# Banded attention in a gated mix kernel: the band as a 0/1 multiply by GpSimd in place of a mask matmul, in attention steps 4 to 11

## The chip, the core and the metric

The kernel runs on one core of one Trainium2 chip. The metric is the time of one execution in device microseconds (us), lower is better. Instructions of the five engines are named as the profile names them: PE is TensorE's matmul and PEld its weight load, DVE is VectorE, ACT is ScalarE, POOL is GpSimd, SP is SyncE, which here only issues DMAs. L596 is line 596 of the kernel before.

## What is computed

Two branches are mixed by a gate. Branch A is a long causal convolution by FFT (H3), branch B is a dilated sliding-window attention: each query sees 8 keys, at distances 0, 2, ..., 14, in 32 heads of 20 columns. The change lies in branch B. Cut to that:

```
def _B_ref(x, wqkv, wo):
    B, S, D = x.shape                    # 1, 2048, 640
    H = 32; Dh = D // H
    W, dil = 8, 2
    qkv = (x @ wqkv) split into q, k, v of H heads
    idx = arange(S)[:, None] - (arange(W) * dil)[None, :]
    mask = idx >= 0
    logits = einsum("bhsd,bhswd->bhsw", q, k[idx]) * Dh ** -0.5
    attn = softmax(where(mask, logits, -1e9))
    o = einsum("bhsw,bhswd->bhsd", attn, v[idx])
    return o.reshape(B, S, D) @ wo

g = sigmoid((A_q * gate_w).sum(-1))
return g * _A_ref(A_q, ...) + (1 - g) * _B_ref(A_q, B_wqkv, B_wo)
```

## The kernel before, in words

**Tiling of the attention.** Even and odd positions are separate sequences, so that the dilated window becomes 8 neighbouring keys. Each sequence is cut into blocks of 57 queries (QB) with the 64 keys (KB) that they can see. For every block and head a 64 x 57 square of scores is computed, of which only a diagonal band of 8 keys per query counts. What lies outside the band has to be made zero before the product with v.

**The unit of work.** A *half* is two heads (of a group of four, t = 0 to 7) over 6 pairs of blocks (a group of blocks, gi = 0 to 2). There are 48 halves, two to a *step*, 24 steps, in the order of `steps` (L575): the groups 0 and 1 with t = 0, 1, then 2, 3, then 4 to 7, and then group 2. For half i, `scores(i)` (L581) issues on PE two mask matmuls of 128 x 342 (L587), whose product of two small factors `mk` and `mq` is 0 in the band and at most -256 outside of it, then 24 score matmuls of 20 rows x 57 columns (L593) that add the scores to it in PSUM tile `sc` (two buffers). ACT then takes the exponential of the 128 x 684 tile into one of four buffers `ET` (L596): outside the band that gives zero. `pv(i)` (L598) multiplies it with v, whose extra column of ones gives the sum for the softmax, in 24 matmuls (L615) into PSUM tile `O` (one buffer); after the second half of a step DVE divides (L622, L625).

**The order of the work.** All of it is written by hand; every engine runs its own instructions in program order and waits on semaphores for the others. In loop k (L703) the order is: `scores(2k+2)`, `fill(0)`, `scores(2k+3)`, `fill(1)`, `pv(2k)`, `fill(2)`, `pv(2k+1)`, `fill(3)`. So the exponentials of a step are needed one loop later. `fill` spreads other work of PE, given by `plan` (L694), over the four places: for k = 0 to 7 the projection of q and k for the other heads (`late_qk`, 5 or 4 units of five matmuls, L349), for k = 8 to 11 that of v (`late_v`, 3 units, L292), from k = 12 on the output projection and the first FFT stages.

**What else hangs on this stage.** On DVE `kv_gen` (L244), the elementwise part of branch A, goes on until k = 2; its last instructions are L257 and L259 (tile `kvo`). When it is done, the tile `kq1` takes the place of what `kv_gen` read (`new_kq(1)`, L752); heads 20 to 31 are moved into it by `send_rest(ft)` (L356), 28 DMAs on SP's queue: ft = 0 to 2 at once (17 DMAs), ft = 3 and ft = 4 when their projection is done, with two loads `hn` of 512 KB (L522) put in between (`load_hn`, L758 and L759). These heads are used from t = 5 on, that is from half 18. GpSimd is nearly empty: small DMAs at the start (L227 to L239), four memsets (L571), 12 small stores and 4 loads of the gate (L725), and output stores at the end.

Of the kernel before, what the change touches and what calls it, by code (L numbers as in the profile page):

```python
# [11 lines left out]
BF = mybir.dt.bfloat16  # L12
F32 = mybir.dt.float32
ACT = mybir.ActivationFunctionType
ALU = mybir.AluOpType
# [4 lines left out]
D = 640  # L20
L = 4096
H = 32
DH = 20
NDT = 5
SCALE = float(DH) ** -0.5

QB = 57
KB = 64
CB = QB + KB
# [7 lines left out]
NMB = 6  # L37
# [5 lines left out]
def _np_bf16(a):  # L43
    return np.asarray(a, dtype=np.float32).astype(ml_dtypes.bfloat16)
# [32 lines left out]
def attn_consts():  # L77
    B, C = 256.0, 512.0
    kk = np.arange(KB); qq = np.arange(QB)
    kc = kk // 8 - 4; ko = kk % 8; qc = qq // 8 - 4; qo = qq % 8  # L80
    sk = np.where(kc % 2 == 0, 1.0, -1.0); sq = np.where(qc % 2 == 0, 1.0, -1.0)
    mk = np.zeros((NF, KB)); mq = np.zeros((NF, QB))
    mk[0] = kc * kc; mk[1] = kc; mk[2] = 1.0
    mq[0] = -B; mq[1] = B * (2 * qc + 1); mq[2] = -B * (qc * qc + qc) - C / 2
    for v in range(8):
        mk[3 + v] = sk * (ko == v)
        mq[3 + v] = (C / 2) * sq * np.where(v < qo, -1.0, 1.0)
    tot = np.einsum("fk,fq->kq", mk, mq)
    dlt = kk[:, None] - qq[None, :]
    inb = (dlt >= 0) & (dlt <= 7)  # L90
    assert (tot[inb] == 0).all() and (tot[~inb] <= -C / 2).all()
    for m in (mk, mq):
        assert (_np_bf16(m).astype(np.float64) == m).all()
    mkz = np.zeros((4, 32, 128)); mqz = np.zeros((4, 32, NMB * QB))
    mkz[:, 0:NF] = np.tile(mk, (1, 2)); mqz[:, 0:NF] = np.tile(mq, (1, NMB))
    sidx = 2 * np.arange(18)[None, :] + (np.arange(128)[:, None] // KB)
    pos = QB * (sidx % NSB) - PRE + (np.arange(128)[:, None] % KB)
    valid = ((pos >= 0) & (pos < 1024)).astype(np.float32)
    return dict(mk=_np_bf16(mkz.reshape(128, -1)), mq=_np_bf16(mqz.reshape(128, -1)), valid=_np_bf16(valid), ident=_np_bf16(np.eye(128)))


def xrow(si, kk):
# [32 lines left out]
def kernel(  # L135
# [14 lines left out]
    nc = tc.nc  # L150
# [8 lines left out]
    ca = {k: nc.inline_tensor(v, name=f"ca_{k}") for k, v in attn_consts().items()}  # L159
# [6 lines left out]
    ident = p0.tile([128, 128], BF, name="ident")  # L166
# [16 lines left out]
    pC = sC.enter_context(tc.tile_pool(name="pC", bufs=1, side="left", reuse_waits="tile"))  # L183
    xTn = pC.tile([128, NDT, 2, XP], BF, name="xTn")
    Wp = pC.tile([128, NDT, 2, NDT, 4, 32], BF, name="Wp")
    WV = pC.tile([128, NDT, D + 8], BF, name="WV")
    valid = pC.tile([128, 18], BF, name="valid")
    sV = ExitStack()
    pV = sV.enter_context(tc.tile_pool(name="pV", bufs=1, side="left", reuse_waits="tile"))
    wl = pV.tile([128, 4, D], BF, name="wl")  # L190
# [46 lines left out]
    nc.gpsimd.dma_start(F1b[:], cf["F1b"].ap())  # L237
    nc.gpsimd.dma_start(mk[:], ca["mk"].ap())
    nc.gpsimd.dma_start(mq[:], ca["mq"].ap())  # L239


    kvs = kv_scr[:]
# [324 lines left out]
    NET = 4  # L567
    ETs = []
    for e in range(NET):
        ETb = pD.tile([128, 2, 352], BF, name=f"ET{e}")  # L570
        nc.gpsimd.memset(ETb[:, :, NMB * QB:352], 1.0)  # L571
        ETs.append(ETb)
    pa_ = ExitStack()
    ppa = pa_.enter_context(tc.tile_pool(name="ppa", bufs=2, space=PSUM, reuse_waits="tile"))
# [6 lines left out]
    def scores(i):  # L581
        gi, t, hf = halves[i]
        kqt = kq[t // 4]
        sc = ppa.tile([128, 2, 512], F32, name="sc", tag="sc")
        for hh in range(2):
            r = 32 * (2 * hf + hh)
            nc.tensor.matmul(sc[:, hh, 0:NW], lhsT=mk[:], rhs=mq[:], start=True, stop=False, skip_group_check=True)  # L587
        for mb in range(NMB):
            for sub in range(2):
                si = 2 * (NMB * gi + mb) + sub  # L590
                for hh in range(2):
                    r = 32 * (2 * hf + hh)
                    nc.tensor.matmul(sc[64 * sub:64 * sub + 64, hh, QB * mb:QB * mb + QB], lhsT=kqt[r:r + DH, t % 4, si, 0:KB],  # L593
                                     rhs=kqt[r:r + DH, t % 4, si, KB:CB], start=False, stop=True,
                                     tile_position=(r, 64 * sub), skip_group_check=True)
        nc.scalar.activation(ETs[i % NET][:, :, 0:NW], sc[:, :, 0:NW], ACT.Exp, scale=SCALE)  # L596

    def pv(i):  # L598
        gi, t, hf = halves[i]
        if hf == 0:  # L600
            Ot = ppa.tile([128, 2, 512], F32, name="O", tag="O", bufs=1)
            Os[(gi, t)] = Ot
            if t == 0:
                oSb = pD.tile([128, 2, 3, D], BF, name="oS", tag="oS", bufs=2)
                oSs[gi] = oSb
        O = Os[(gi, t)]
        ET = ETs[i % NET]
        for mp in range(3):
            for hh in range(2):
                for par in range(2):  # L610
                    for s in range(2):
                        mb = 2 * mp + par
                        sl = mp * 4 + 2 * hf + hh
                        rows = slice(64 * s, 64 * s + 64)
                        nc.tensor.matmul(O[64 * par:64 * par + 64, s, 21 * sl:21 * sl + 21],  # L615
                                         lhsT=ET[rows, hh, QB * mb:QB * mb + 64],
                                         rhs=VW[rows, NMB * gi + mb, 4 * t + 2 * hf + hh, :], start=True, stop=True,
                                         tile_position=(64 * s, 64 * par), skip_group_check=True)
        if hf == 1:
            Ov = O[:, :, 0:252].rearrange("p a (s e) -> p a s e", e=21)  # L620
            rd = pD.tile([128, 2, 12], F32, name="rd", tag="rd", bufs=2)
            nc.vector.reciprocal(rd[:], Ov[:, :, :, DH])  # L622
            for s in range(2):
                dst = oSs[gi][:, s, :, 4 * DH * t:4 * DH * (t + 1)].rearrange("p b (h d) -> p b h d", h=4)
                nc.vector.tensor_tensor(dst, Ov[:, s, :, 0:DH].rearrange("p (b h) d -> p b h d", h=4),  # L625
                                        rd[:, s].rearrange("p (b h) -> p b h", h=4).unsqueeze(3).to_broadcast([128, 3, 4, DH]),
                                        ALU.mult)
# [75 lines left out]
    for k in range(len(steps)):  # L703
        late_eng[:] = "aa" if k < 5 else "da"
        if k == 12:
            gl = gate()
            sC.close()
            pF = ctx.enter_context(tc.tile_pool(name="pF", bufs=1, side="left", reuse_waits="tile"))
            kv = pF.tile([128, 2, 64, 80], BF, name="kv")
            G = pF.tile([128, 32, 2, 128], BF, name="G")  # L710
            for c in range(2):
                for h in range(2):
                    for q in (0, 2, 1, 3):
                        paced.append((kv[32 * q:32 * q + 32, c, 32 * h:32 * h + 32],
                                      raw(kvs, (2 * q + c) * S * 80 + 2560 * h, [[64 * 80, 32], [1, 2560]])))
            for a_ in range(0, 32, 8):
                for q in (0, 2, 1, 3):
                    paced.append((G[32 * q:32 * q + 32, a_:a_ + 8],
                                  cf["G"].ap()[32 * q:32 * q + 32, a_ * 256:a_ * 256 + 2048].rearrange("p (a r b) -> p a r b", a=8, r=2)))
            fg["s"] = itertools.chain(s1_gen(("h", 0), 0, True), s1_gen(("h", 1), 1, True))  # L720
        if k == 12:
            fg["o"] = op_gen(0)
        if k == 14:
            for a_ in gl:
                nc.gpsimd.dma_start(*a_)  # L725
        if k == 16:
            fg["p"] = op_gen(1)
        units = [c for c, n in plan.get(k, []) for _ in range(n)]
        cut = [len(units) * j // 4 for j in range(5)]

        def fill(j):
            for c in units[cut[j]:cut[j + 1]]:
                advance(fg[c], 1)

        nxt = k + 1 < len(steps)
        if nxt:
            scores(2 * k + 2)
        fill(0)
        if nxt:
            scores(2 * k + 3)  # L740
        fill(1)
        pv(2 * k)
        fill(2)
        pv(2 * k + 1)
        fill(3)
        if k < KC:
            advance(kvg, 3)
        if k == KC - 1:
            while advance(kvg, 1):
                pass  # L750
            sV.close()
            new_kq(1)  # L752
            for ft in range(2 + sum(plan[k_][0][1] for k_ in range(KC)) // 12):
                send_rest(ft)
            hb = p0.tile([128, 16 * D], BF, name="hb", tag="hT")
            hT = hb[:].rearrange("p (g m i) -> p g m i", g=NG, i=IL)
            bl = hb[:].rearrange("p (t d) -> p t d", d=D)
            load_hn(0)  # L758
            load_hn(1)  # L759
        if k > 8:  # L760
            advance(ht, 2 if k < 16 else 3)
# [155 lines left out]
```

## Time and profile before

| what | value |
|---|---|
| time, median of 4 runs | 302.88 us (301.67, 302.47, 303.29, 305.65) |
| the profiled execution | 301.67 us |
| its span, first to last instruction | 299.9 us |
| mean granted TensorE clock | 0.916 |
| PE busy | 245.8 us, 82% |
| DVE busy | 196.6 us, 66% |
| ACT busy | 180.4 us, 60% |
| GpSimd busy | 26.6 us, 9% |
| PE busy from 72 to 111 us, loops 3 to 10 | 37.22 of 39.00 us |
| ACT, DVE, GpSimd busy in the same stretch | 20.16, 20.25, 0.00 us |
| mask matmuls, L587 | 96, 22.9 us busy |

Times in the profile are counted from the span's start. Busy time of PE overlaps, because matmuls are pipelined: what an instruction costs is read from where the next one starts, not from its duration. An engine's idle time is put down to what ended it ("<-"). GpSimd's durations are rough.

### The profile page before, as it was taken

How to read it: one execution, taken by the hardware profiler on the slowest of the kernel's cores; microseconds unless marked ns; L12 is line 12 of the kernel's file. 1: busy time of each engine (PE TensorE's matmuls, PEld its weight loads, DVE VectorE, ACT ScalarE, POOL GpSimd, SP SyncE). 2: the span in 40 equal slices, each digit the busy share in tenths (PEclk: the TensorE clock that was granted, in tenths of full speed). 3: DMA queues.
4: the chain of work that ended last, by engine and by line, in shares of the span. 5: the costliest groups of instructions: out<-in, count | busy, mean ns of one | idle time of the engine just before them, and what ended most of it. 6: DMA issues, size and time to landing. Idle time of an engine off the chain costs nothing. (4 is left out here: it accounts for less than half of the span.)

```text
span 299.9 us, 12166 instructions
## 1 busy us (share of the span) xinstructions
PE 245.8 (82%) x5502; PEld 177.6 (59%) x5502; DVE 196.6 (66%) x294; ACT 180.4 (60%) x275; POOL 26.6 (9%) x52
## 2 busy tenths in 40 slices
PE   2788999999999979987699987899787969597420
PEld 1556766566566646654456654587676969497310
DVE  2587999299343668757497554025868877985771
ACT  2366788666655444542245653398778977975860
POOL 3820004100000001320000000000000000000232
PEclk9999999999999999996959999599889979979655
DMA  6999905120556630464622324562855949491273
GB/s 190 357 357 406 341 2 156 46 91 2 126 94 121 134 45 21 101 169 119 145 66 65 107 63 128 153 154 68 195 166 116 240 83 242 106 256 40 71 198 90
DMA packets 19162, 42.22 MB, mean 141 GB/s; under 512 B 4263, under 2 KB 11767, under 8 KB 18102
## 3 DMA queue, kind: packets, MB, share of 16 engines
q1 hardware_dynamic: 17606, 39.19, 47.7%
q0 software_dynamic: 1504, 2.24, 3.1%
q8 instruction: 43, 0.70, 1.1%
q14 instruction: 9, 0.07, 0.1%
HBM read 26.22 MB, written 7.87 MB: 114 GB/s over the span
## 5 line engine op out<-in xcount | busy, mean ns | idle before, releaser
L596 ACT ACTIVATE ET<-sc 128x684 bf16<-128x684 f32 x48 | 35.3, 742 | 25.2 <-PE sc L593 25.0
L349 PE MATMUL pj<-xTn,Wp 128*128 128x349 bf16 (+1 forms) x300 | 49.9, 311 | 0.0
L463 PE MATMUL s<-Am,G 64*128 64x64 bf16 x1280 | 25.6, 197 | 11.1 <-issue 4.9
L349 PEld LDWEIGHTS <-Wp 128*128 128x128 bf16 x300 | 26.6, 97 | 12.8
L122 ACT CAST kq<-pj 128x342 bf16<-128x342 f32 (+1 forms) x54 | 24.0, 473 | 16.6 <-PE pj L349 16.3
L463 PEld LDWEIGHTS <-G 64*128 64x128 bf16 x1280 | 22.7, 100 | 15.1 <-issue 9.7
L496 DVE TENSOR_TENSOR Hb<-Up,Hb 128x1024 bf16<-128x1024 bf16 x40 | 25.1, 686 | 4.3 <-ACT Up L122 1.8
L122 ACT CAST Am<-s 128x1024 bf16<-128x1024 f32 x25 | 24.7, 1040 | 3.8 <-PE s L439 3.7
L652 PE MATMUL op<-wo,oT 128*128 128x320 bf16 x120 | 22.5, 327 | 5.0 <-ACT oT L639 2.2
L122 ACT CAST Hb<-s 128x1024 bf16<-128x1024 f32 x20 | 20.0, 1020 | 10.5 <-PE s L463 10.3
L509 PE MATMUL i<-M,Hb 128*128 128x128 bf16 x320 | 23.7, 234 | 2.2 <-DVE Hb L496 2.0
L509 PEld LDWEIGHTS <-Hb 128*128 128x128 bf16 x320 | 22.7, 150 | 3.3 <-DVE Hb L496 3.1
L657 DVE CAST fin<-op 128x320 bf16<-128x320 f32 x24 | 11.7, 486 | 19.2 <-PE op L652 12.0
L593 PEld LDWEIGHTS <-kq 20*64 20x64 bf16 x1152 | 13.9, 109 | 16.6 <-issue 15.6
L587 PE MATMUL sc<-mq,mk 128*128 128x342 bf16 x96 | 22.9, 322 | 0.2 <-ACT ET L596 0.2
L250 DVE TENSOR_TENSOR pr<-kvw,wl 128x2560 bf16<-128x2560 bf16 x16 | 22.9, 1486 | 0.1
L615 PEld LDWEIGHTS <-ET 64*64 64x64 bf16 x1152 | 13.9, 111 | 12.4 <-issue 11.5
L593 PE MATMUL sc<-kq 20*64 20x57 bf16 x1152 | 19.4, 195 | 1.8 <-issue 1.3
L292 PEld LDWEIGHTS <-vw 128*128 128x128 bf16 x180 | 16.9, 100 | 6.6
L528 DVE STREAM_TRANSPOSE hb<-hn 128x512 bf16<-128x512 bf16 x20 | 19.9, 1040 | 0.2
L615 PE MATMUL O<-VW,ET 64*64 64x21 bf16 x1152 | 18.6, 182 | 0.1
L625 DVE TENSOR_TENSOR oS<-O,rd 128x240 bf16<-128x240 f32 x48 | 17.3, 403 | 0.9
(71 smaller groups left out, 370.0 us busy)
## 6 DMA issues: line engine op xcount, KB each, us to landing
Hb<-Hb SPq DMA_DIRECT2D x10, 512.0 KB
xN<-in_A_q_dram SPq DMA_DIRECT2D x4, 640.0 KB
kvw<-in_A_k_dram SPq DMA_DIRECT2D x4, 640.0 KB
kv_scr<-kvo SPq DMA_DIRECT2D x4, 640.0 KB
hn<-in_A_ssm_k_dram SPq DMA_DIRECT2D x5, 512.0 KB
kv<-kv_scr SPq DMA_DIRECT2D x16, 160.0 KB
qg<-in_A_q_dram SPq DMA_DIRECT2D x16, 160.0 KB
b_scr<-fin SPq DMA_DIRECT2D x36, 60.0 KB
```

The source lines that it names most:

```text
L122: self.nc.scalar.copy(dst, src)
L250: nc.vector.tensor_tensor(pr[:, j].rearrange("p (n c) -> p n c", n=4), kh[:, 4 * c + 3 - j:4 * c + 7 - j, :], wl[:, j, :].unsqueeze(1).to_ ...
L349: nc.tensor.matmul(ps[:, 0:n], lhsT=Wp[:, dt, which, ft].rearrange("p h c -> p (h c)"), rhs=xTn[:, dt, c // 3, a:a + n], start=(dt == 0), ...
L463: nc.tensor.matmul(o, lhsT=G[rows, j, r, :], rhs=Am[rows, 2 * j + r, :, :], start=(r == 0), stop=(r == 1), tile_position=(64 * c, 0), skip ...
L496: nc.vector.tensor_tensor(blk_(H_), blk_(Up), blk_(H_), ALU.mult)
L509: nc.tensor.matmul(o, lhsT=src[:, c, :, :, 8 * oc + il].rearrange("p q j -> p (q j)"), rhs=M[:, k, :], start=(k == 0), stop=(k == 1), skip ...
L528: nc.vector.transpose(hT[:, g].rearrange("p (c n) i -> p n c i", c=2)[:, 16 * p:16 * p + 16], hnb[0][:, g % 2].rearrange("p (a n) -> p n a ...
L587: nc.tensor.matmul(sc[:, hh, 0:NW], lhsT=mk[:], rhs=mq[:], start=True, stop=False, skip_group_check=True)
L593: nc.tensor.matmul(sc[64 * sub:64 * sub + 64, hh, QB * mb:QB * mb + QB], lhsT=kqt[r:r + DH, t % 4, si, 0:KB], rhs=kqt[r:r + DH, t % 4, si, ...
L596: nc.scalar.activation(ETs[i % NET][:, :, 0:NW], sc[:, :, 0:NW], ACT.Exp, scale=SCALE)
L615: nc.tensor.matmul(O[64 * par:64 * par + 64, s, 21 * sl:21 * sl + 21], lhsT=ET[rows, hh, QB * mb:QB * mb + 64], rhs=VW[rows, NMB * gi + mb ...
L652: nc.tensor.matmul(op[:, 0:320], lhsT=oTs[j][:, ft, :], rhs=wo[:, ft, 320 * hf:320 * hf + 320], start=(ft == 0), stop=(ft == NDT - 1))
```

## The change

In halves 8 to 23 (steps 4 to 11) the two mask matmuls are left out, and the score matmuls start their own sums instead of adding to the mask. The exponential is then taken of all scores, and GpSimd multiplies the result in place by `band`, a constant of 0 and 1 of 128 x 342 that is used for both heads of a half. `times_band(i)` stands in loop k after `fill(1)` for half 2k+2 and after `fill(3)` for half 2k+3; on GpSimd's queue only the order counts. The constant comes with one more DMA on GpSimd's queue at the start. To find room for it, tile `WV` loses 6 unused columns of each of 5 rows and the `ET` buffers 2 columns of each of 2 rows. Halves 0 to 7 and 24 to 47 stay as they are.

```
-    return dict(mk=..., mq=..., valid=..., ident=...)
+    band = np.tile(inb.astype(np.float32), (2, NMB))
+    return dict(band=_np_bf16(band), mk=..., mq=..., valid=..., ident=...)
...
-    WV = pC.tile([128, NDT, D + 8], BF, name="WV")
+    WV = pC.tile([128, NDT, D + 2], BF, name="WV")
     valid = pC.tile([128, 18], BF, name="valid")
+    band = pC.tile([128, NMB * QB], BF, name="band")
...
     nc.gpsimd.dma_start(mq[:], ca["mq"].ap())
+    nc.gpsimd.dma_start(band[:], ca["band"].ap())
...
-        ETb = pD.tile([128, 2, 352], BF, name=f"ET{e}")
-        nc.gpsimd.memset(ETb[:, :, NMB * QB:352], 1.0)
+        ETb = pD.tile([128, 2, 350], BF, name=f"ET{e}")
+        nc.gpsimd.memset(ETb[:, :, NMB * QB:350], 1.0)
...
-        for hh in range(2):
-            r = 32 * (2 * hf + hh)
+        eng = by_band(i)
+        for hh in range(0 if eng else 2):
             nc.tensor.matmul(sc[:, hh, 0:NW], lhsT=mk[:], rhs=mq[:], start=True, stop=False, skip_group_check=True)
...
-                                     rhs=kqt[r:r + DH, t % 4, si, KB:CB], start=False, stop=True,
+                                     rhs=kqt[r:r + DH, t % 4, si, KB:CB], start=eng is not None, stop=True,
...
+    def by_band(i):
+        return nc.gpsimd if 8 <= i < 24 else None
+
+    def times_band(i):
+        if i < len(halves) and by_band(i):
+            ET = ETs[i % NET][:, :, 0:NW]
+            by_band(i).tensor_tensor(ET, ET, band[:].unsqueeze(1).to_broadcast([128, 2, NW]), ALU.mult)
...
         fill(1)
+        times_band(2 * k + 2)
         pv(2 * k)
         fill(2)
         pv(2 * k + 1)
         fill(3)
+        times_band(2 * k + 3)
```

More of the change, by code (lines that the diff above doesn't have):

```diff
@@ L98, in attn_consts @@
     valid = ((pos >= 0) & (pos < 1024)).astype(np.float32)
-    return dict(mk=_np_bf16(mkz.reshape(128, -1)), mq=_np_bf16(mqz.reshape(128, -1)), valid=_np_bf16(valid), ident=_np_bf16(np.eye(128)))
+    band = np.tile(inb.astype(np.float32), (2, NMB))
+    return dict(band=_np_bf16(band), mk=_np_bf16(mkz.reshape(128, -1)), mq=_np_bf16(mqz.reshape(128, -1)), valid=_np_bf16(valid), ident=_np_bf16(np.eye(128)))
 def xrow(si, kk):
```

## Prediction

> **What bounds the kernel now.** I read the page first, then the timelines of PE, SP and DVE over the stage of the change, the waits of SP's queue, and the clock by windows. The chain that ended last reaches back only to 214.30 us, so what bounds loops 3 to 10 (72 to 111 us) is read from the timelines. The page:
>
> ```profile
> PE   2788999999999979987699987899787969597420
> PEclk9999999999999999996959999599889979979655
> ...
> L596 ACT ACTIVATE ET<-sc 128x684 bf16<-128x684 f32 x48 | 35.3, 742 | 25.2 <-PE sc L593 25.0
> ...
> L587 PE MATMUL sc<-mq,mk 128*128 128x342 bf16 x96 | 22.9, 322 | 0.2 <-ACT ET L596 0.2
> ...
> L593 PE MATMUL sc<-kq 20*64 20x57 bf16 x1152 | 19.4, 195 | 1.8 <-issue 1.3
> ```
>
> One slice is 7.5 us: PE is full from the sixth slice to the fourteenth and ACT waits 25.0 us for PE's scores. So PE looks like the bound and the masks like part of it. But in the last line score matmuls wait 1.8 us, and the groups of 72 to 126 us put 0.5 of it down to DMA kq<-kq. PE's timeline shows where:
>
> ```profile
> 103.93 0.46 PE L587 MATMUL sc<-mq,mk 128*128 128x342 bf16 x2
> 104.32 0.59 PE L593 MATMUL sc<-kq 20*64 20x57 bf16 x24
> ...
> 108.41 0.46 PE L587 MATMUL sc<-mq,mk 128*128 128x342 bf16 x2
> 110.16 0.18 PE L593 MATMUL sc<-kq 20*64 20x57 bf16 x1 [1.29 <-issue]
> 110.84 0.50 PE L593 MATMUL sc<-kq 20*64 20x57 bf16 x23 [0.49 <-DMA kq<-kq]
> 111.27 0.85 PE L292 MATMUL pv<-WV,vw 128*128 128x320 bf16 x5
> ```
>
> Counting loops, 103.93 is half 21 and 108.41 is half 23, the last of the change. Half 23 stands from about 108.8 to 110.84 until its heads' rows have landed. Half 21 is already on the edge: its scores take 0.59 us where others take 0.38, and its weight loads at 104.32 were released by kq<-kq. Are these transfers late because PE is? SP's timeline, and a row of its waits:
>
> ```profile
> 63.21 13.82 SPq L263 DMA_DIRECT2D kv_scr<-kvo  x2
> 77.13 14.28 SPq L363 DMA_DIRECT2D kq<-kq  x17
> 91.45 1.60 SPq L522 DMA_DIRECT2D hn<-in_A_ssm_k_dram  x2
> 93.16 12.94 SPq L363 DMA_DIRECT2D kq<-kq  x11
> ```
>
> ```profile
> SPq L363 <- DMA hn<-in_A_ssm_k_dram: 2.3, 1, 2.3
> ```
>
> SP issues without a pause from 77.13 to 96.87 (17 + 2 + 5 DMAs, 0.82 us each). It waits for the last projection (ft = 4) until 99.62, issues two, and then waits 2.3 us, to 103.25, for a load hn to land. The last four go from 103.25 to 106.1 and land by 110.84. The start at 77.13 is DVE's doing:
>
> ```profile
> 73.00 0.72 DVE L625 TENSOR_TENSOR oS<-O,rd 128x240 bf16<-128x240 f32 x2
> 73.64 1.48 DVE L257 TENSOR_TENSOR pr<-pr 128x2560 bf16<-128x2560 bf16 x1
> 75.16 1.49 DVE L259 TENSOR_TENSOR kvo<-pr,vab 128x2560 bf16<-128x2560 bf16 x1
> ```
>
> DVE has no gap from 60.18 to 76.65, and all it did there comes before half 8. So the arrival of the rows hangs on kvo (76.65), on SP's issue and on the hn load. None of these gets earlier when PE does.
>
> **What the skill says.** (1) GPSIMD Engine Reference, section 3.1: a two-input tensor_tensor of 2048 elements takes GpSimd 4497 ns, 2.2 ns an element. The trace before has no such instruction. (2) SBUF — State Buffer, section "SBUF: two separate sides": GpSimd and a DVE instruction with two SBUF inputs share a port pair as an exclusive lock; whoever starts first has it for the whole instruction. The trace has one overlap:
>
> ```profile
> 8.86 2.73 POOL L233 COPY VW<-valid 128x576 bf16<-128x576 bf16 x1 [5.45 <-DMA valid<-ca_valid]
> ```
>
> ```profile
> 9.04 1.69 DVE L286 COPY vw<-xTn 128x640 bf16<-128x640 bf16 x4
> ```
>
> DVE's four copies kept the 0.48 us that they take elsewhere, GpSimd ended 0.86 us after the last: GpSimd seems to have stood back, though it began first. (3) TensorE: Matmul & The Clock Gate, Part 1: windows of 3.4 us decide PE's clock; an idle one halves it. Here less is enough: PE was busy 1.54 us of 133.60 to 137.02, and the clock was 0.50 for the next 6.83 us. 106.30 to 109.70, busy 2.58, was not punished.
>
> **Removed.** What a mask pair costs, from PE's timeline:
>
> ```profile
> 76.76 1.65 PE L349 MATMUL pj<-xTn,Wp 128*128 128x349 bf16 x10
> 78.25 0.45 PE L587 MATMUL sc<-mq,mk 128*128 128x342 bf16 x2
> 78.63 0.38 PE L593 MATMUL sc<-kq 20*64 20x57 bf16 x24
> ```
>
> The pair holds the scores back by 78.63 - 78.25 = 0.38 us. About 0.085 of this is the change from wide to small tiles and stays: ten projections take 78.25 - 76.76 = 1.49, so five 0.745, but from such five to a pv it is 81.23 - 80.40 = 0.83. So a pair is worth 0.295 us, and 0.38 where the half follows another's scores directly (19, 21, 23: loops 8 to 10 have no fill there). Sum: 13 x 0.295 + 3 x 0.38 = 5.0 us, 4.3 of it up to the scores of half 21 (12 x 0.295 + 2 x 0.38).
>
> **Where it goes.** Half 21's scores would be ready to start at 104.32 - 4.3 = 100.0; their rows come at about 104.3. These 4.3 us turn into a wait. After that halves 22 and 23 save another 0.7, against the wait that ends at 110.84. No mask is removed behind 110.84. So of 5.0 us nothing reaches the end: 0.
>
> **Clock.** The new idle 4.3 us around 100 to 104.3 leaves at least one clock window emptier than the one that was punished, so I expect half clock for some 6.8 us from about 103 to 105 on. Between the scores of halves 21 and 23 lie three v units (at half clock 1.49 instead of 0.85, from the like L652 at 139.53), two pv (0.51 for 0.37) and one set of scores (0.54 for 0.38): 3 x 0.64 + 2 x 0.14 + 0.16 = 2.4 us more, less 0.7 for the masks. Half 23 would be reached at 108.8 + 1.7 = 110.5, while its rows land at 110.16 and 110.84. Cost 0 to 0.3; if the half clock lasts longer, 1 to 2. I take 0.3.
>
> **Added on GpSimd.** 16 multiplies of 128 x 684. By the skill's price 684 x 2.2 = 1.5 us each, 24 in all (an estimate). By the trace's copy 2.73 / 576 = 4.74 ns an element, 3.24 us, as the upper end; its 0.86 us behind the copies would make it 1.02, the lower. I take 1.5, since that row is of this operation. A pair of halves takes PE 5.2 us in loops 4 to 7 less 0.6, and 4.4 less 0.7 in loops 8 to 10; two multiplies, 3.0 us, fit into both. pv(8) comes at about 80.1 (81.23 less four pairs), and with a start at 76.7 the product is done at 78.2. It costs nothing; cover gone, pv waits on PE's queue, with all projections behind it. pv now waits for GpSimd in place of ACT: no wait is added to PE.
>
> **Queues.** Band's DMA (87.5 KB) stands behind mq at 18.5 us; at the 400 GB/s of that stretch it delays loads by 0.2 us, covered: no engine waits for a load between 20 and 72 us. The first six gate stores (3.65 us at 49.60) move behind the 16 multiplies, to about 114; the other six wait for the last v unit at 118.79 anyhow, so the gate is at most 1 us later, and used behind 200 us. The shorter memsets and tiles: 0.
>
> **Sum.** 0 + 0.3: span 299.9 to 300.2, time 302.0 for that execution. It lay 1.2 below the median of its runs, so 303.2 as a median.
>
> **Rivals.** *GpSimd is the bound* (slower). Multiply n is done at 76.7 + n T, and pv(23), the sixteenth, was at 117.41: above T = 2.54 us it decides (pv(17) gives 2.6). At 3.24 us it ends at 128.5, 11 us late: 314. For it: the 4.74 ns copy; against: that copy overlapped DVE's. *The lock delays kvo.* The first exponential ends at about 73.7, between L257 (73.64) and L259 (75.16). If GpSimd gets the pair at 75.12, kvo, SP's chain and half 23's rows are one multiply later, 1.5 us, or 3 if the second also goes first: 304.7 to 306.2. Against: DVE follows itself in 0.04 us, and the overlap at 9 us. *The gain survives* (faster): if rows come earlier with PE, up to 5.0 us: 297.9; half of it: 300.4. For it: ft = 4 would be projected 3 us earlier; against: SP has that much backlog, and hn decides. *The clock* stays halved after 111: 305.
>
> **Numbers.** Forecast 0.55, lock 0.17, GpSimd bound 0.13, gain 0.10, clock 0.05. The forecast's own range is 301.5 to 304.8, from the runs' spread. Below 300 lies most of the gain, above 308 the GpSimd case: that leaves 0.2 out. Over 1% (3 us, about what can be told from no change): faster 0.09; slower 0.27, from GpSimd, the lock's upper part and some clock; within 0.64.
>
> **What would show it.** Right: mask matmuls 64, not 96; half 21's scores wait some 4 us for kq<-kq; half 23's still start near 110.8; kvo ends at 76.65; multiplies near 1.5 us; a half-clock stretch between 103 and 112. Wrong: kvo later than 77, pv waiting for GpSimd, or half 23 before 109.

## The result, and the profile after

The changed kernel takes 305.88 us (median of 11 runs, 303.3 to 310.9), the kernel before in the same comparison 303.94 us (16 runs): ratio 1.0211, 95% interval [1.0146, 1.0276]. The ratio is formed from the fast runs of each kernel alone, those within 1.5% of its fastest (4 of the 16 before, 7 after), while the two medians of all runs differ by 0.6% only. Two later comparisons of the same two kernels gave less: 1.004 [0.9908, 1.0172] and 1.0074 [0.9983, 1.0165]; a third (a3) has no ratio, and its medians, 307.16 and 301.52, differ by 1.9%. So the change makes the kernel slower, by something between nothing and 2%; forecast were 303.2 us, 0.3 more than before. The profiled execution took 305.88 us, its span 304.1, 4.2 us more than before. Line numbers are 3 to 13 higher than in the kernel before: L587 is now L590, L593 is L596, L596 is L599, and the multiply is L607.

From the page, the rows that answer to those of before:

```profile
PE   2788999999999499986598986798778879587520
...
PEclk9999999999999857999959999799799959997975
...
L599 ACT ACTIVATE ET<-sc 128x684 bf16<-128x684 f32 x48 | 35.2, 742 | 22.6 <-PE sc L596 21.9
...
L607 POOL TENSOR_TENSOR ET<-ET,band 128x684 bf16<-128x684 bf16 x16 | 24.7, 1560 | 40.2 <-ACT ET L599 40.1
```

The fourteenth slice (98.8 to 106.4 us) was full of matmuls and now is a 4; the clock is an 8 there and a 5 and a 7 in the two slices after it. ACT still waits 21.9 us for PE. GpSimd works 24.7 us, less than PE's steps leave it. The hole in PE's timeline:

```profile
100.21 0.38 PE L596 MATMUL sc<-kq 20*64 20x57 bf16 x25
104.75 0.53 PE L596 MATMUL sc<-kq 20*64 20x57 bf16 x23 [4.16 <-DMA kq<-kq]
105.22 1.52 PE L295 MATMUL pv<-WV,vw 128*128 128x321 bf16 x5
...
111.33 0.54 PE L596 MATMUL sc<-kq 20*64 20x57 bf16 x23 [0.35 <-DMA kq<-kq]
...
117.60 0.54 PE L596 MATMUL sc<-kq 20*64 20x57 bf16 x24
```

At 100.21 are half 20 and one matmul of half 21, at 104.75 the rest of half 21 after 4.16 us of waiting for its rows, at 111.33 half 23, at 117.60 half 24. Before, half 20's exponential started at 104.11; now it starts at 100.71, 3.4 us earlier: most of the masks' time was really saved (the forecast's sum up to there, 12 x 0.295 + 0.38, is 3.9). Half 23, at 110.84 before, is no earlier. From the windows (length, then busy time and count of PE, PEld, DVE, ACT, POOL, then PE's clock, the DMA share and GB/s):

```profile
101.00:104.44 3.44, 0.00 (x0) 0.00 (x0) 0.41 (x2) 0.45 (x1) 1.40 (x1) 1.00 0.56 139
104.44:118.09 13.65, 12.98 (x224) 7.14 (x225) 7.24 (x16) 3.69 (x9) 7.59 (x9) 0.50 0.25 35
```

After 3.44 us without a matmul the clock is 0.50 for 13.65 us, in which PE is busy 12.98. And DVE's timeline around kvo, then GpSimd's first rows there:

```profile
73.81 1.48 DVE L260 TENSOR_TENSOR pr<-pr 128x2560 bf16<-128x2560 bf16 x1
75.33 2.58 DVE L262 TENSOR_TENSOR kvo<-pr,vab 128x2560 bf16<-128x2560 bf16 x1
```

```profile
73.91 8.09 POOL L607 TENSOR_TENSOR ET<-ET,band 128x684 bf16<-128x684 bf16 x4 [24.11 <-ACT ET L599]
83.83 2.77 POOL L607 TENSOR_TENSOR ET<-ET,band 128x684 bf16<-128x684 bf16 x2 [1.82 <-ACT ET L599]
```

kvo takes 2.58 us instead of 1.49, and SP's first row DMA moves from 77.13 to 78.39. The first two of the four multiplies at 73.91 took 2.65 and 2.64 us; the other 14 took 1.40 or 1.41.

### The profile page after: what moved, and what is told of

It is laid out like the page before. It is cut to its first block, busy times and chain, and to the rows that moved or that the text cites. A ratio compares the mean times of both kernels' runs of the same rounds, so it can differ in the third digit from the quotient of the medians.

```text
span 304.1 us, 12123 instructions
## 1 busy us (share of the span) xinstructions
PE 243.1 (80%) x5470; PEld 175.4 (58%) x5470; DVE 197.4 (65%) x294; ACT 179.4 (59%) x275; POOL 52.8 (17%) x69
## 4 chain that ended last, share of the span: by engine, by line
PE 53%; DMA 16%; DVE 10%; ACT 8%; SPq 5%; issue 4%; POOL 1%; DVEq 0%; POOLq 0%; ACTq 0%
PE pj L352 15%; PE i L512 6%; DMA b_scr<-fin 6%; PE psv L295 6%; DMA kq<-kq 5%; DVE Hb L499 4%; PE op L663 4%; PE s L466 3%; PE sc L596 3%; SPq L657 3%; PE O L626 3%; PE s L442 3%; DMA Hb<-Hb 2%; PE sc L590 2%; PE pv L295 2%
## 5 line engine op out<-in xcount | busy, mean ns | idle before, releaser
L599 ACT ACTIVATE ET<-sc 128x684 bf16<-128x684 f32 x48 | 35.2, 742 | 22.6 <-PE sc L596 21.9
L466 PE MATMUL s<-Am,G 64*128 64x64 bf16 x1280 | 23.8, 192 | 13.3 <-issue 6.2
L607 POOL TENSOR_TENSOR ET<-ET,band 128x684 bf16<-128x684 bf16 x16 | 24.7, 1560 | 40.2 <-ACT ET L599 40.1
L466 PEld LDWEIGHTS <-G 64*128 64x128 bf16 x1280 | 21.1, 96 | 16.9 <-issue 10.9
L512 PE MATMUL i<-M,Hb 128*128 128x128 bf16 x320 | 25.6, 245 | 4.3 <-DVE Hb L499 4.1
L123 ACT CAST Am<-s 128x1024 bf16<-128x1024 f32 x25 | 24.7, 1042 | 5.7 <-PE s L442 5.6
L512 PEld LDWEIGHTS <-Hb 128*128 128x128 bf16 x320 | 24.4, 152 | 5.5 <-DVE Hb L499 5.3
L663 PE MATMUL op<-wo,oT 128*128 128x320 bf16 x120 | 20.7, 307 | 6.1 <-DVE fin L668 2.6
L898 POOL DMA_DIRECT2D out_dram<-qg x12 | 6.0, 499 | 108.3 <-DVE qg L896 108.2
L596 PEld LDWEIGHTS <-kq 20*64 20x64 bf16 x1152 | 14.1, 111 | 18.5 <-issue 13.0
L295 PEld LDWEIGHTS <-vw 128*128 128x128 bf16 x180 | 18.2, 107 | 8.9 <-DVE vw L289 0.4
L596 PE MATMUL sc<-kq 20*64 20x57 bf16 x1152 | 19.3, 198 | 4.5 <-DMA kq<-kq 4.5
```

Of the source, the lines that this page charges most:

```text
L123: self.nc.scalar.copy(dst, src)
L295: nc.tensor.matmul(ps[:, 0:320 + a], lhsT=vw[:, dt].rearrange("p b k -> p (b k)"), rhs=WV[:, dt, 320 * a:320 * a + 320 + a], start=(dt == ...
L466: nc.tensor.matmul(o, lhsT=G[rows, j, r, :], rhs=Am[rows, 2 * j + r, :, :], start=(r == 0), stop=(r == 1), tile_position=(64 * c, 0), skip ...
L512: nc.tensor.matmul(o, lhsT=src[:, c, :, :, 8 * oc + il].rearrange("p q j -> p (q j)"), rhs=M[:, k, :], start=(k == 0), stop=(k == 1), skip ...
L607: by_band(i).tensor_tensor(ET, ET, band[:].unsqueeze(1).to_broadcast([128, 2, NW]), ALU.mult)
L663: nc.tensor.matmul(op[:, 0:320], lhsT=oTs[j][:, ft, :], rhs=wo[:, ft, 320 * hf:320 * hf + 320], start=(ft == 0), stop=(ft == NDT - 1))
```

## The experiments

**The theories.** *T1, late rows*: PE's saving is void because half 21 waits for the rows; the multiply delays kvo and with it the rows, and the hole brings half clock. *T2, the clock alone*: rows arrive as before, and the half clock is the loss. *T3, the multiplies* cost by themselves, as load on ports or buffers. *T4, noise*: the 2% are the scatter of executions.

**How the runs are compared.** Run medians scatter by some 2%, so the table also has two lengths from each profiled execution: "stage" is from half 8's exponential to half 24's, "rest" from half 24's to the end of the span. All multiplies and all the masks left out but half 8's lie in the stage; half 8's lies just ahead of it, so that leaving it out starts the stage 0.3 us earlier and makes it that much longer. The rest is 185.2 us in the mean of all 18 profiles, with a standard deviation of 2.1, and follows no variant that the table shows clearly. Wait is the longest that scores made for rows (which half). Ratios are to the kernel before in the same comparison; in one of the four later comparisons (a3, e1b, e2b, e9) none was formed, and its "before" had a median of 301.52.

| kernel | median us | ratio [95%] | kvo us | wait us | stage | rest |
|---|---|---|---|---|---|---|
| before | 303.94 | | 1.49 | 1.29 (23) | 41.8 | 184.9 |
| before again (b2) | 305.62 | 1.0055 [0.9957, 1.0154] | 1.49 | 2.87 (18) | 44.0 | 185.6 |
| after | 305.88 | 1.0211 [1.0146, 1.0276] | 2.58 | 4.16 (21) | 45.2 | 185.9 |
| after again (a2) | 305.04 | 1.004 [0.9908, 1.0172] | 2.58 | 6.57 (21) | 45.4 | 184.8 |
| after again (a3) | 307.16 | | 2.58 | 10.51 (21) | 47.9 | 182.1 |
| after again (a4) | 305.55 | 1.0074 [0.9983, 1.0165] | 2.58 | 7.43 (21) | 46.1 | 188.4 |
| gate stores first (e8) | 305.40 | 0.9977 [0.985, 1.0105] | 2.57 | 9.54 (21) | 47.4 | 183.3 |
| masks and multiplies (e3) | 307.91 | 1.0108 [1.0033, 1.0182] | 2.58 | 3.21 (18) | 46.0 | 186.8 |
| PE kept busy (e1) | 305.86 | 0.9924 [0.9806, 1.0043] | 2.58 | 0.89 (23) | 40.5 | 184.5 |
| the same (e1b) | 305.17 | | 2.58 | 4.82 (21) | 46.4 | 185.1 |
| no multiplies (e2) | 302.24 | 0.9936 [0.9869, 1.0002] | 1.49 | 2.72 (19) | 42.7 | 182.5 |
| the same (e2b) | 302.06 | | 1.49 | 6.06 (21) | 43.5 | 185.6 |
| the same (e2c) | 304.48 | 1.0067 [0.9985, 1.0148] | 1.49 | 5.88 (21) | 43.3 | 185.6 |
| from half 10 (e6) | 307.80 | 1.0108 [1.0044, 1.0172] | 1.49 | 3.82 (19) | 42.9 | 188.3 |
| hn later, before (e5) | 299.39 | 0.9922 [0.9832, 1.0013] | 1.49 | none | 39.4 | 183.4 |
| hn later, after (e4) | 296.96 | 0.9836 [0.9746, 0.9926] | 2.58 | none | 35.9 | 185.7 |
| hn later, no multiplies (e9) | 294.49 | | 1.49 | 0.16 (23) | 35.3 | 182.1 |
| hn later, from half 10 (e10) | 299.12 | 0.9843 [0.9743, 0.9942] | 1.49 | 0.66 (23) | 36.1 | 189.3 |

### PE kept busy while it would wait (e1, e1b)

Tells T1 from T2: work without use fills the hole. The change with this in `scores`, after the mask matmuls:

```
+        for hh in range(26 if i == 21 else 0):
+            nc.tensor.matmul(sc[:, hh % 2, 0:NW], lhsT=mk[:], rhs=mq[:], start=True, stop=True, ...)
```

> The changed kernel with 26 mask matmuls (3.8 us at full clock) put ahead of the scores of half 21 into the same PSUM tile, which the scores then overwrite: PE computes them for nothing while it would stand waiting for kq<-kq. Theory (the idle 4.2 us halve the clock from 104 to 118 us): no half clock before 120 us, half 24's exponential near 116 us (118.24 in the changed kernel, 115.01 before), ratio to before 1.000 to 1.005. Rival (the time goes to GpSimd's multiplies or to the lock on DVE): half 24 stays near 118 us or later, ratio 1.02.

> The changed kernel with 26 mask matmuls for nothing ahead of half 21's scores, a second time. Theory (the idle time at half 21 halves the clock, and that costs 2 to 3 us on top of the rows): half 23's exponential follows the landing of its rows at once, and half 24 follows half 23 by 3.6 us in place of 6.3; faster than a3_after by 0.5 to 1%. Rival (the half clock is hidden, because half 23's rows are late anyhow): no faster than a3_after.

PE's timeline of the first (the script's lines are 2 higher behind the edit):

```profile
101.25 3.94 PE L592 MATMUL sc<-mq,mk 128*128 128x342 bf16 x26
105.12 0.38 PE L598 MATMUL sc<-kq 20*64 20x57 bf16 x24
```

The hole is filled, half 21 runs at full clock (0.38 us, not 0.53), and the stage is 40.5 us, the shortest of all kernels with the loads in their old place. The rows were as early there as in the first profile of the change: the last row DMA went out at 105.64 us, there at 105.73. In the second profile the rows came so late that half 21 still waited 4.82 us, half clock followed (108.6 to 115.4), and the stage was 46.4: the hole was not filled, so this profile says nothing of what filling it is worth. The medians, 305.86 and 305.17, are those of the changed kernel.

So the half clock comes from the hole, and with early rows it costs what the first profile of the change shows. It costs something with late rows too. In a2 PE has no wait at all between half 21 and half 23, and still works at half clock for most of that way:

```profile
109.36 1.52 PE L295 MATMUL pv<-WV,vw 128*128 128x321 bf16 x5
...
114.58 0.69 PE L596 MATMUL sc<-kq 20*64 20x57 bf16 x48
```

and the same way in the kernel before:

```profile
104.85 0.86 PE L292 MATMUL pv<-WV,vw 128*128 128x321 bf16 x5
...
107.71 0.45 PE L587 MATMUL sc<-mq,mk 128*128 128x342 bf16 x2
```

From the end of half 21's scores to half 22's work these are 5.22 us instead of 2.87, and 4.51, 5.22 and 4.43 in a3, a4 and e8. Most of this is not lost, because the last row lands late there: by the semaphore updates in the traces at 114.2, 116.6, 114.6 and 115.6 us. Half 23's exponential follows that landing by 1.6, 1.1, 1.7 and 1.0 us, where it takes 0.7 or 0.8 when PE stands waiting for the row (first profiles of before and after): up to 1 us is left to the clock. And the kernels without multiplies below have the same slow stretch (5.22, 4.72 and 4.83 us). T2 is thus part of why the saved time does not come out, but not what sets the changed kernel apart from these.

### No multiplies (e2, e2b, e2c), and both (e3)

`times_band` does nothing (e2, where the band DMA and the smaller tiles stay, so that these aren't what is tested), or the masks stay and the multiplies are made as well (e3):

```
-        if i < len(halves) and by_band(i):
+        if False:
```

```
-        for hh in range(0 if eng else 2):
+        for hh in range(2):
...
-   ... start=eng is not None, stop=True,
+   ... start=False, stop=True,
```

> The changed kernel without GpSimd's multiplies: no mask and no band in halves 8 to 23, so the attention of these heads sums over all keys of a block. Theory: kvo ends about 1.1 us earlier (76.8), half 21 still waits about 3.3 us for kq<-kq, the clock is still halved behind it, half 24 starts 1 us earlier than in the changed kernel at most (117.2 to 118.2), ratio to before 1.01 to 1.02. Rival (the multiplies cost the time): half 24 near 114 us, ratio 0.99 to 1.00.

> The changed kernel without GpSimd's multiplies, no band and no mask in halves 8 to 23, a second time. Theory: kvo takes 1.49 us, so the rows start 1.1 us earlier, and the rest of a3_after stays: 0.2 to 0.6% faster than a3_after. Rival (the multiplies cost more than the one lock): over 1% faster.

> The changed kernel without the multiplies (no mask and no band in halves 8 to 23), third time. Theory: ratio 0.99 to 1.005, half 23 within 2 us of b2_before. Rival (multiplies slow the transfers): half 23 3 us or more ahead of a4_after.

> The changed kernel with the mask matmuls back in halves 8 to 23 and the multiplies kept (they multiply zeros and finished values, so the output stays). Theory: kvo is late by 1.1 us, half 23 by 0.5 to 1 us, PE has no long idle time at half 21 and so no half clock before 120 us: half 24 near 116 us, ratio 1.000 to 1.006. Rival (multiplies): half 24 near 118 us, ratio 1.02.

DVE's timeline of e2:

```profile
76.19 1.49 DVE L262 TENSOR_TENSOR kvo<-pr,vab 128x2560 bf16<-128x2560 bf16 x1
```

kvo is back at 1.49 us in all three. Their stage is 42.7, 43.5 and 43.3 us, that of the kernel before 41.8 and 44.0: 5.0 us of mask time less on PE is worth nothing there, as the prediction said. The first run's own expectation, a ratio of 1.01 to 1.02, was missed: 0.9936, where its rival had put it. With the multiplies the stage is 45.2 to 47.9 in the five profiles of the changed kernel (e8 among them), mean 46.4. So the multiplies cost about 3.2 us in the stage (46.4 less 43.2). The run times point the same way, more weakly: the 18 runs of the three kernels without them have a mean of 303.1 us, 29 of the changed kernel 305.7, standard errors 0.6 each, but these come from different comparisons. In the two that had both, the means differ by 3.4 (a3, e2b) and 1.0 us (a4, e2c).

Where the 3.2 us lie can be read from the same profiles. From half 8's exponential to half 21's the means are 36.4 and 33.8 us, so 2.5 us come with half 21's rows, kvo's 1.09 included. From half 21's to half 24's they are 10.0 and 9.3, and the difference is the first profile's alone: 12.85 there, 9.2 to 9.4 in the other four, 9.3 to 9.4 without multiplies.

e3 missed its expectation. The masks should have kept PE late enough to have no hole, but half 18, the first to use the new tile, already waited 3.21 us for rows, and the stage was 46.0 us, as in the changed kernel. In these profiles masks on or off make no difference where rows are late; multiplies on or off do.

### The first steps left out (e6)

If the multiplies cost through kvo, only those of halves 8 and 9 matter, since all others run after it:

```
-        return nc.gpsimd if 8 <= i < 24 else None
+        return nc.gpsimd if 10 <= i < 24 else None
```

> The changed kernel with the band by GpSimd from half 10 on and masks for halves 8 and 9, so that no multiply meets DVE's last two instructions of kv_gen. Theory: kvo takes 1.49 us in place of 2.58 and ends near 76.8, half 23's rows are there about 0.5 to 1 us earlier; half 21 waits about 2.6 us, which still halves the clock: half 24 at 116.5 to 117.8 us, ratio 1.005 to 1.02. Rival (the lock is the main loss): half 24 near 115 us, ratio 1.00.

kvo took 1.49 us, and the stage 42.9 us, though 14 of the 16 multiplies are there: that of e2, not that of the changed kernel. So in the stage the cost of the multiplies is the collision at kvo, and not their load (T3). But the median is 307.8 us. Some of this lies outside of the profiled work: e6's runs are 2.8 to 3.5 us longer than their spans from first to last instruction, those of the other kernels 1.7 to 1.9 (e10, with the same edit, 2.0 to 3.4); no run shows why. By span e6's median is 304.75 us, the kernel before in that comparison 304.7. The rest was long too, 188.3 us, one of the three longest of all profiles, and e10 has the longest, 189.3. Whether that is scatter or a cost of the edit further on isn't settled by two profiles; what e6 shows is the stage, in one profile, not a faster kernel.

### The same kernels again (a2, a3, a4, b2), and the gate stores (e8)

Unchanged kernels, for T4:

> The changed kernel again, unchanged, as the control of this group on the same chip: half 21 waits 3 to 5 us for kq<-kq, kvo takes about 2.6 us, a half-clock stretch begins within 5 us of that wait, ratio to before 1.005 to 1.025.

> The changed kernel once more, as the control of a group that asks how large each loss is. Half 21 waits 3 to 9 us for kq<-kq, as long as the rows of that execution take, and a half-clock stretch follows. Ratio to before 1.00 to 1.02.

> The changed kernel, in one group with a profile of the kernel before. Theory: half 23's exponential 0.5 to 3 us later than in b2_before, of which 1.1 us is kvo and the rest the spread of the transfers; ratio 1.00 to 1.015. Rival: 4 us or more later, ratio 1.02.

> The kernel before, profiled a second time. Theory (the rows are late by their own transfers, whatever GpSimd does): the loads hn take 8 to 14 us and half 21 or 23 waits for rows here too, the longer the later hn lands; half 23's exponential at 111 to 117 us; ratio 1.00. Rival (the multiplies slow the transfers): half 23 within 1.5 us of the first profile's 111.44.

The waits of half 21 in a2 and a3, 6.57 and 10.51 us, are longer than expected. From a3's PE timeline and windows:

```profile
111.61 0.53 PE L596 MATMUL sc<-kq 20*64 20x57 bf16 x23 [10.51 <-DMA kq<-kq]
112.07 1.52 PE L295 MATMUL pv<-WV,vw 128*128 128x321 bf16 x5
```

```profile
105.38:115.68 10.30, 4.07 (x79) 2.29 (x81) 0.66 (x2) 1.23 (x3) 1.40 (x1) 0.50 0.52 95
```

Most of that half clock lies inside the wait. And the kernel before also had a hole in its second profile:

```profile
99.83 0.35 PE L593 MATMUL sc<-kq 20*64 20x57 bf16 x19
103.05 0.24 PE L593 MATMUL sc<-kq 20*64 20x57 bf16 x5 [2.87 <-issue]
105.11 1.52 PE L292 MATMUL pv<-WV,vw 128*128 128x321 bf16 x5
```

Half 18 of the unchanged kernel is held back for 2.87 us between its matmuls, and the clock is halved from 104.8 to 108.3. The profile names no releaser ("issue"); the position, in the first half that uses the rows, is my reason for counting it as a wait for them. So the profile that the prediction was read from was an execution with early rows, and the arrival of the rows is itself a scattering quantity. What scatters is seen in SP's wait for the loads hn in the first profile of the change, which was a short one:

```profile
SPq L366 <- DMA hn<-in_A_ssm_k_dram: 4.5, 2, 3.2
```

That sum was 2.3 and 3.5 us in the two profiles of before, 5.7 to 6.1 without multiplies and in e6, and 4.5, 6.6, 7.3, 7.9 and 8.7 in the five of the changed kernel. Without masks SP reaches the wait earlier, because the projection of ft = 4 is done earlier; but that holds with and without multiplies, so what lies between 5.7 to 6.1 and 6.6 to 8.7 is later landing. The spread is as large as that difference, though: in the changed kernel's first profile and in e1, both with the multiplies, the last row DMAs go out earlier after kvo's end (27.8 and 27.6 us) than in any profile without them that has the loads in their old place (28.7 to 31.2).

In e8 the first six gate stores go out ahead of the multiplies, where they were before the change:

```
+    for a_ in gate()[:6]:
+        nc.gpsimd.dma_start(*a_)
...
-            for a_ in gl:
+            for a_ in gl[6:]:
```

> The changed kernel with the first six gate stores issued ahead of the multiplies on GpSimd's queue, as early as before the change. Theory (rows of kq<-kq and the clock): nothing changes, within 0.5% of a2_after. Rival (the gate stores, moved behind the multiplies to 114 us, disturb the later transfers): 1% or more faster than a2_after, at the level of before.

The stage is 47.4 us with a hole of 9.54: their place in the queue isn't the cause.

### The rows freed from the loads (e4, e5, e9, e10)

If the rows decide, the saving must come out once they are early. The two hn loads (1 MB) are issued at the end of loop 7, behind all rows on SP's queue, and the transposes that need them begin later:

```
+        if k == 7:
             load_hn(0)
             load_hn(1)
-        if k > 8:
-            advance(ht, 2 if k < 16 else 3)
+        if k > 10:
+            advance(ht, 2 if k < 13 else 3)
```

e4 is the change with this, e5 the kernel before, e9 the change without multiplies, e10 the change from half 10.

> The changed kernel with the two hn loads moved behind the last kq<-kq rows on SP's queue (issued at the end of loop 7) and the transposes that read them begun two loops later. Theory (the rows that half 21 to 23 wait for hold up PE, and hn holds up the rows): the rows of half 21 are there by 100 us, half 23 does not wait or under 1.5 us, no half clock before 125 us, half 24's exponential at 109.5 to 112 us, ratio to before 0.975 to 0.99. Rival (the multiplies are what costs): half 24 not before 115 us, ratio 1.00 or more.

> The kernel before with the same move of the hn loads, masks kept, no band: the control for what the move gives alone. Theory: half 23's wait of 2 us goes, half 24 near 113 us, ratio to before 0.985 to 1.00, and the version with the band is 3 to 5 us faster than this one. Rival (multiplies cost): the version with the band is no faster than this one.

> The version with the hn loads moved behind the rows, without GpSimd's multiplies (no band and no mask in halves 8 to 23): what the 16 multiplies cost where PE waits for no rows. Theory: kvo ends 1.1 us earlier but nothing waits for it, so half 24 stands at 110 us counted from the same start as with multiplies, within 0.5 us, and the time within 0.5% of the ratio of 0.984 that the version with multiplies had. Rival: ratio 0.97 or less.

> The version with the hn loads moved behind the rows and the band by GpSimd from half 10 on only, masks in halves 8 and 9, so that kvo meets no multiply. Theory: kvo takes 1.49 us, but nothing waits for the rows there, and two mask pairs (0.6 us) come back: the same as with the band from half 8, ratio 0.975 to 0.99.

SP's and PE's timelines of e4:

```profile
79.58 22.77 SPq L366 DMA_DIRECT2D kq<-kq  x28
102.39 1.34 SPq L525 DMA_DIRECT2D hn<-in_A_ssm_k_dram  x2
```

```profile
101.40 0.70 PE L596 MATMUL sc<-kq 20*64 20x57 bf16 x48
...
105.10 0.85 PE L596 MATMUL sc<-kq 20*64 20x57 bf16 x48
...
109.27 0.45 PE L590 MATMUL sc<-mq,mk 128*128 128x342 bf16 x2
```

All 28 row DMAs go out in one piece, 22.77 / 28 = 0.81 us each, and halves 20 to 23 follow without a wait, at full clock. The stage is 35.9 us in e4 and 39.4 in e5: 3.6 of the 5.0 us now come out (3.9, with the 0.3 us of half 8's mask ahead of the stage). The medians are 296.96 and 299.39; e4 is 0.9836 [0.9746, 0.9926] of the kernel before, so with the rows freed the changed kernel is faster than the kernel before; the move without the change (e5) gives 0.9922, and the two intervals overlap. Without multiplies the stage is 35.3 and from half 10 36.1: in these profiles, where halves wait for rows little or not at all, the same multiplies and the same 2.58 us for kvo cost 0.6 us at most. T1 is what this fits, with the half clock (T2) as a smaller part of the loss. It is shown by the groups of profiles, not by each one: the arrival of the rows scatters by more than kvo's 1.09 us, and in e1 they were early although kvo was late.

## Why the prediction was wrong

It held most of the way, and its result failed on two terms.

**Right: the saving and where it goes.** 64 mask matmuls, half 20 earlier by 3.4 us, half 21 waiting 4.16 us for kq<-kq (forecast 4.3), half 23 no earlier. That 4.16 is so near is luck in part: in the four other profiles of the changed kernel it was 6.6 to 10.5. The experiments go further than the forecast: without multiplies the stage is no shorter than before (42.7 to 43.5 against 41.8 and 44.0), and with early rows the masks' time does come out.

**Right: GpSimd isn't the bound.** The multiply alone takes 1.40 us, forecast 1.5; that is 2.05 ns an element in bf16, near the 2.2 worked out from the fp32 row of the Trainium skill's GPSIMD Engine Reference, section 3.1. The 4.74 ns of the copy at 9 us, kept as the upper end, did not hold for this operation; whether that copy was waiting isn't shown. In all, pv's weight loads waited for a product twice, 0.8 us together.

**Wrong: "If GpSimd gets the pair at 75.12" was held for a rival, against it "DVE follows itself in 0.04 us, and the overlap at 9 us".** It happened in every profile with a multiply there (eight of 2.57 or 2.58 us, and e4), and never without one. The durations show how. L260 runs from 73.81 to 75.29, the first multiply from 73.91 to 76.56, kvo from 75.33 to 77.91, the second multiply from 76.53 to 79.17. If the first multiply waits for L260 and then runs, it runs 76.56 less 75.29 = 1.27 us; kvo waits 2.58 less 1.49 = 1.09 of them; the second multiply waits for kvo and runs 1.26. e3, where the masks put the first multiply later beside L260, has it too:

```profile
74.74 1.48 DVE L260 TENSOR_TENSOR pr<-pr 128x2560 bf16<-128x2560 bf16 x1
75.13 2.36 POOL L607 TENSOR_TENSOR ET<-ET,band 128x684 bf16<-128x684 bf16 x1 [24.39 <-ACT ET L599]
76.26 2.58 DVE L262 TENSOR_TENSOR kvo<-pr,vab 128x2560 bf16<-128x2560 bf16 x1
```

The multiply begins 0.39 us into L260 instead of 0.10, is shorter by that much, and again ends 1.27 us after L260, which keeps its 1.48 us. So the two don't share at a lower speed: one stands while the other runs. That agrees with the exclusive lock of the Trainium skill, SBUF — State Buffer, section "SBUF: two separate sides". What no row before showed is who gets the pair when one engine waits and the other has its next instruction ready: here the waiting GpSimd, ahead of DVE's next. The overlap at 9 us was the wrong guide: those DVE instructions were copies with one input, not two, only one GpSimd instruction was concerned, and DVE's keeping its pace was read as DVE winning.

The rival's price of 1.5 us for kvo was nearly right (1.09), but the effect is larger than its first link. In the stage the multiplies cost 3.2 us (46.4 less 43.2), and nothing when the two at kvo are left out (42.9). Of the 2.1 us beyond kvo, 1.4 come before half 21's exponential, with rows that land later, and 0.7 are the half clock of the first profile. That the rival's time, 304.7 to 306.2, holds the measured 305.88 is therefore luck in part.

**Wrong in size: the half clock, "Cost 0 to 0.3; if the half clock lasts longer, 1 to 2. I take 0.3".** The slower work itself was summed rightly: three v units and two pv took 5.22 us instead of 2.87, 2.35 more, and half 23 came so late by it that it waited 0.35 us for its rows. What failed is the length, behind half 23. The forecast took 6.8 us of half clock, the length of the stretch around 137 in the trace before. In the profiled execution it was 13.65 us, and half 24 came 6.27 us after half 23 (117.60 less 111.33) instead of 3.57: 2.7 us, more than half of that execution's 4.2. It isn't the usual case: in a2, a3, a4 and e8 the same step took 3.2 to 3.8 us, since half 23 itself came 4 to 6 us later and the half clock had ended. So the two terms partly replace each other: with early rows the clock costs, with late rows mainly the rows do.

**What the 2% are.** The stage gives 46.4 us in five profiles after and 42.9 in two before: +3.5 us, 1.2% (0.3 of it from the earlier start of the stage). The ratios give 0.4 to 2.1%. T4 doesn't explain the stage, but it does explain why comparisons of the same two kernels differ as much, since the rest alone scatters by 2.1 us. The forecast's own range, 301.5 to 304.8, did not hold the time of 305.88; the wider one over the rivals, 300 to 308, did.

**Still open.** Why the same transfers land up to 7 us apart in different executions; why a half clock lasted 3.4, 6.8, 10.2 or 13.65 us; why the rows land later by more than kvo's own delay in most profiles with the multiplies; and the long rest of e6 and e10, and their time outside of the span.

## What to carry to other kernels

Removing work from a busy engine pays only up to the next arrival that doesn't depend on it: PE was 95% busy here, and 5 us less of work brought nothing until the rows were moved ahead of 1 MB of loads on their queue. Before putting work on GpSimd, look at which two-input DVE instruction it can start beside, and at what hangs on that instruction's end: one multiply of 1.40 us delayed one 1.49 us instruction by 1.09 us, and a chain of 28 transfers hung on it, though the delays seen in single executions vary by more than that. And read a wait's edge from more than one execution: in the first profile of the kernel before half 23 waited for its rows, in the second half 18, twice as long.

## What the hardware showed that was not expected

- A GpSimd multiply of 128x684 in bf16 takes 1.40 us alone and 2.65 us when it starts beside a two-input DVE instruction; DVE's instruction behind it goes from 1.49 to 2.58 us.
- Every half-clock stretch in the 18 profiles but the last of each, which runs on past the end of the span, lasted 3.41, 6.83, 10.24 or 13.65 us: one to four times the same length (96 stretches). After a hole of 3.44 us PE stayed at half clock for 13.65 us although it was busy for 12.98 of them. The Trainium skill, TensorE: Matmul & The Clock Gate, Part 1, says that one busy window of some 3.4 us brings the full clock back. In the second profile of the kernel before the half clock ended after 3.4 us; in this one it did not, and the measurement decides.
- Two loads of 512 KB among 28 DMAs of rows on the same queue held the last rows back by amounts that differ between executions: the last row DMA began 27.8 to 34.3 us after kvo's end in the five profiles of the changed kernel, with the same program order.
